# Bonus-term sums of twelve chunks moved from VectorE to TensorE, with a new instruction order

## The chip, the cores and the metric

One core of a Trainium2 chip runs the kernel. The metric is device time in microseconds (us). TensorE (PE) multiplies matrices, VectorE (DVE), ScalarE (ACT) and GpSimd (POOL) work element by element, and SyncE (SP) issues the transfers (DMA). Each engine runs its own instructions in the order in which they were written. All on-chip operands are spread over 128 partitions.

## The reference

The program is a recurrence, a mixture of attention experts and a two-layer network, for 4 batches, 8 heads, 768 time steps and 48 dimensions per head. Only the recurrence is touched:

```python
for t in range(S):
    kt, vt, rt, wt = (k[:, :, t], v[:, :, t], r[:, :, t], w[:, :, t])
    cur = np.einsum('bhd,bhe->bhde', u[None] * kt, vt)
    y[:, :, t] = np.einsum('bhd,bhde->bhe', rt, state + cur)
    state = wt[:, :, :, None] * state + np.einsum('bhd,bhe->bhde', kt, vt)
```

The part with `cur` is the bonus term. It equals v times one number for each time step and head: the sum over d of r·u·k. That number is called cb here.

## The kernel before, in words

Time is cut into chunks of 128 steps: 6 chunks for each batch, 24 in all, numbered n = 0 to 23. For each chunk SP loads w (L615), k (L623), r (L627) and v (L631) into one buffer `seq`, of which there are two. In `seq`, r, k and w lie transposed: the 48 dimensions of the even head of a pair stand in partitions 0 to 47, those of the odd head in 64 to 111, the other partitions hold zeros in r and k, and the 4 pairs times 128 steps run along the row. A further load brings r and k again in token order (128 steps in the partitions, 384 columns each) into `tok`, of which there is one (L636).

Work on a chunk:

- DVE scans the decays backward and forward (`scan` L641, `forth` L653), and multiplies them into k (`mk_k2`, L672) and r (`mk_rp`, L677).
- PE forms the scores (`mm_a`, L717), DVE copies their lower triangle (`am_copy`, L724), and PE adds the state's part (`mm_inter`, L748) and the chunk's own part (`mm_intra`, L757) into one PSUM bank `py`, of which the first 384 of 512 columns are used.
- `mm_k` (L735) transposes k, ACT copies it, `mm_d` (L766) forms the state's update, and DVE adds it (`state`, L777 and L779).
- POOL multiplies r by k in `tok` (`mk_rk`, L681) and the product by u (`mk_ruk`, L691). DVE sums each head's 48 columns (`mk_cb`, L696). POOL multiplies v by that (`mk_cv`, L701), DVE adds it to `py` (`xsum`, L786), and ACT takes absolute values for a later scale (`xabs`, L790).

A `seq` buffer is free for chunk n + 2 when `w_check`, `mm_intra`, `mm_d` and `mk_cv` of chunk n have read it.

After a batch's chunks come its projections (L874, L933), its attention (L1027 to L1135, with transposes by DMA such as `pt<-hl`) and its network (`mm_1` L1228, `mm_2` L1261). Beside the first chunks DVE also unpacks the network's weights (`decode`, L495 to L497) in two-input integer operations.

Nothing of this runs in the order of the source. A planner (class `Plan`) holds for each step an engine, a guessed duration, what it comes after and which buffers it takes and frees. It builds one order for all engines from a table `PLACE` of due times, one for each group of steps, and constants `PRM`. On PE it puts in matmuls without a use (`spin`, L587) where it expects gaps, until 208 us of its own time.

Of the kernel before, what the change touches and what calls it, by code (L numbers as in the profile page):

```python
# [9 lines left out]
F32 = mybir.dt.float32  # L10
# [49 lines left out]
    ('proj', 0): -5466.14, ('proj', 0, 1): 2505.74, ('proj', 1): 261.37, ('proj', 2): -16407.28,  # L60
# [11 lines left out]
    ('vals', 0, 1): 4670.36, ('vals', 1): 5093.45, ('vals', 2): -248.26, ('vals', 3): 10028.19, ('w1', 's'): -5079.13,  # L72
# [10 lines left out]
    'a_hi': -2276.49, 'a_lo': -4079.33, 'a_of': -4548.51, 'a_tr': -7215.53, 'ae': -2249.08, 'am_copy': -1211.61,  # L83
    'f_flag': -3788.23, 'f_rows': -3940.42, 'f_turn': -2958.01, 'forth': -7679.7, 'g_exp': -2732.59,
    'g_norm': -7208.19, 'g_rank': -1849.15, 'hi': 3513.51, 'lo': 2290.0, 'load': -15619.34, 'load_g': -1002.54,
    'load_k': -1514.23, 'load_q': -1834.95, 'load_r': 9715.31, 'load_u': -4843.94, 'load_v': -675.79, 'm_hi': 1044.13,
    'm_lo': -2041.0, 'm_out': 1738.78, 'm_store': -1805.88, 'mk': 828.69, 'mk_begin': -1810.97, 'mk_cb': 5573.98,
    'mk_cv': 1486.88, 'mk_dec': -5704.55, 'mk_k2': 14428.2, 'mk_k2t': 2766.97, 'mk_rk': 1907.93, 'mk_rp': 1676.92,
    'mk_ruk': 484.58, 'mm_1': 5584.91, 'mm_2': 2883.03, 'mm_a': 2028.85, 'mm_av': -3068.64, 'mm_d': 4246.45,
    'mm_inter': -951.53, 'mm_intra': -3321.81, 'mm_k': 4392.85, 'mm_o': -7878.45, 'mm_q': 1795.75, 'mm_s': 1704.41,  # L90
    'mm_v': -3681.48, 'mt': -1390.8, 'n_hi': -6261.32, 'n_lo': 3514.0, 'n_root': 1264.18, 'n_tr': 12577.73,
    'n_var': 2244.75, 'n_xn': -6780.08, 'o1': 1405.65, 'o2': 1686.29, 'o3': -151.85, 'o4': 5380.07, 'o5': 1003.69,
    'o_mean': 648.76, 'o_st': -1580.13, 'o_x1': 1196.05, 'q_hi': 6033.53, 'q_lo': -1025.56, 's_exp': 4056.51,
    's_hi': -10957.04, 's_lo': -1639.03, 's_max': -686.85, 's_tr': -8118.61, 'scan': -1869.51, 'se': 348.87,
    'stack': -322.35, 'state': 522.51, 'times': 1089.39, 'top': 1912.06, 'unpack': -918.54, 'v_hi': -2083.81,
    'v_lo': -2996.08, 'vc': 952.84, 'w_check': 347.52, 'ws_hi': 2045.73, 'ws_lo': -5959.97, 'ws_load': 4116.29,
    'ws_top': -14162.27, 'x_hi': 1895.35, 'x_lo': 9570.84, 'x_tr': 8171.3, 'xabs': -9224.95, 'xsum': -2843.55,
# [192 lines left out]
SPLIT = 1  # L290
RW = 384
# [12 lines left out]
def kernel(  # L304
# [68 lines left out]
    seen = const.tile([P, B * NC], F32, name="seen")  # L373
    V.memset(seen, 0.0)
    sum2 = const.tile([P, NP, max(PRM["NWA"], 1)], F32, name="sum2")
    V.memset(sum2, 0.0)
    decay = const.tile([P, B * NC, NP], F32, name="decay")
    g_sb = const.tile([P, KK], F32, name="g_sb")
    u_sb = const.tile([P, DM], F32, name="u_sb")
    spare = const.tile([P, DM], F8, name="spare")  # L380
    junk = const.tile([P, 512], F8, name="junk")
    low = const.tile([P, E, S], F16, name="low")
    G.memset(low, 0.0)
    wt = {}
    for nm, shape in (("qk", [P, 2, KK, 2 * E * HD]), ("vg", [P, 2, KK, E * HD + E]), ("wo", [P, 2, 2, DM]),
# [211 lines left out]
    def rwkv_chunk(n):  # L597
# [9 lines left out]
        def mine(tag, *more):  # L607
            return (tag, (n,) + more)
# [841 lines left out]
```

## Time and profile before

| | |
|---|---|
| three runs | 703.66, 704.58 and 707.35 us (median 704.58) |
| the profiled execution | 705.03 us, of which the span from first to last instruction is 703.3 us |
| PE matmuls | 647.3 us busy, of which 67.5 us are spins |
| DVE | 524.5 us busy |
| ACT | 396.5 us busy |
| POOL | 94.3 us busy |
| mean granted clock of PE | 0.968 |

Busy times say how much work an engine has, not which engine sets the end. That differs between stages of the span, so the rows below are given by stage. 1.7 us of the profiled execution lie outside the span.

### The profile page before, as it was taken

How to read it: one execution, taken by the hardware profiler on the slowest of the kernel's cores; microseconds unless marked ns; L12 is line 12 of the kernel's file. 1: busy time of each engine (PE TensorE's matmuls, PEld its weight loads, DVE VectorE, ACT ScalarE, POOL GpSimd, SP SyncE). 2: the span in 40 equal slices, each digit the busy share in tenths (PEclk: the TensorE clock that was granted, in tenths of full speed). 3: DMA queues.
4: the chain of work that ended last, by engine and by line, in shares of the span. 5: the costliest groups of instructions: out<-in, count | busy, mean ns of one | idle time of the engine just before them, and what ended most of it. 6: DMA issues, size and time to landing. Idle time of an engine off the chain costs nothing.

```text
span 703.3 us, 15255 instructions
## 1 busy us (share of the span) xinstructions
PE 647.3 (92%) x5599; PEld 473.9 (67%) x5606; DVE 524.5 (75%) x1321; ACT 396.5 (56%) x1176; POOL 94.3 (13%) x113
## 2 busy tenths in 40 slices
PE   7567999978899999999999999999989999999996
PEld 4444765536676786867687768577766777676773
DVE  8999898999899987887888858669764675563321
ACT  4643344879657665567584555586554576553410
POOL 4113411002222122110102200002000000000000
PEclk9867899989999999999999999999999999999998
DMA  8646566526677876756855753446674346353110
GB/s 314 205 129 213 141 156 187 196 66 140 160 165 192 165 162 148 202 92 95 187 108 145 208 126 67 84 101 156 113 118 116 73 91 120 74 79 69 31 46 28
DMA packets 173875, 92.59 MB, mean 132 GB/s; under 512 B 144736, under 2 KB 158048, under 8 KB 173792
## 3 DMA queue, kind: packets, MB, share of 16 engines
q1 hardware_dynamic: 173792, 91.53, 56.3%
q8 instruction: 46, 0.75, 0.5%
q14 instruction: 37, 0.30, 0.1%
HBM read 44.31 MB, written 4.72 MB: 70 GB/s over the span
## 4 chain that ended last, share of the span: by engine, by line
PE 56%; DVE 23%; DMA 14%; issue 3%; ACT 1%; POOL 1%; SPq 0%; DVEq 0%; POOLq 0%
PE pm L1228 16%; PE pz L1261 12%; DMA pt<-hl 7%; PE pq L874 4%; PE pv L933 3%; PE po L1083 3%; PE py L757 3%; PE px L1135 3%; PE pa L717 3%; PE spin L587 3%; DVE junk L1039 2%; DMA xT<-xs 2%; DVE hl L1061 2%; DMA seq<-in_seq_dram 2%; DVE bw L641 2%
## 5 line engine op out<-in xcount | busy, mean ns | idle before, releaser
L1228 PE MATMUL pm<-xnT,w_w 128*128 128x256 f16 x1296 | 155.5, 274 | 4.4 <-DMA xnT<-x 3.2
L1261 PE MATMUL pz<-w_w,hid 128*128 128x384 f16 x864 | 151.6, 326 | 0.6 <-DVE hid L1243 0.6
L1228 PEld LDWEIGHTS <-w_w 128*128 128x128 f16 x1296 | 123.7, 98 | 21.6 <-DMA xnT<-x 3.6
L1261 PEld LDWEIGHTS <-hid 128*128 128x128 f16 x864 | 81.8, 98 | 49.3 <-issue 0.7
L1047 ACT ACTIVATE ps<-ps,bias,scales 128x512 f32<-128x512 f32 (+3 forms) x128 | 76.7, 599 | 63.6 <-DVE junk L1039 63.2
L1039 DVE TENSOR_SCALAR_CACHE_REDUCE junk<-ps,scales 128x512 fp8e4<-128x512 f32 (+3 forms) x96 | 58.8, 613 | 22.1 <-PE ps L1028 11.7
L1061 DVE SCALAR_TENSOR_TENSOR hl<-ps,hl 128x512 f16<-128x512 f32 (+3 forms) x128 | 61.2, 501 | 16.6 <-ACT hl L1056 15.8
L587 PE MATMUL spin<-starts,ident 128*128 128x512 bf16 x241 | 67.5, 422 | 3.1 <-POOL ident masks.py:199 2.1
L1243 DVE SCALAR_TENSOR_TENSOR hid<-pm,hid 128x512 f16<-128x512 f32 x72 | 49.3, 685 | 24.5 <-ACT hid L1239 24.2
L1239 ACT ACTIVATE hid<-pm 128x512 f16<-128x512 f32 x72 | 42.6, 594 | 40.9 <-PE pm L1228 40.5
L1056 ACT ACTIVATE hl<-ps 128x512 f16<-128x512 f32 (+3 forms) x128 | 53.2, 447 | 13.3 <-DMA pt<-hl 11.9
L1083 PE MATMUL po<-vt,pt 128*128 128x64 f16 x1008 | 44.9, 194 | 12.4 <-DMA pt<-hl 12.1
L1083 PEld LDWEIGHTS <-pt 128*128 128x128 f16 x1008 | 39.7, 99 | 24.2 <-DMA pt<-hl 20.1
L874 PE MATMUL pq<-xT,w_qk 128*128 128x384 f16 x288 | 49.4, 326 | 1.2 <-DVE lg L946 0.8
L701 POOL TENSOR_TENSOR cv<-seq,cb 128x384 f32<-128x384 f32 x24 | 24.1, 1004 | 182.2 <-ACT cv L790 58.7
L757 PE MATMUL py<-seq,am 128*128 128x48 f32 x384 | 46.5, 273 | 1.8 <-DVE am L724 1.8
L757 PEld LDWEIGHTS py<-seq,am 128*128 128x128 f32 x384 | 45.5, 192 | 3.2 <-DVE am L724 2.0
L587 PEld LDWEIGHTS <-ident 128*128 128x128 bf16 x248 | 25.3, 106 | 31.7 <-issue 10.8
L1177 POOL TENSOR_TENSOR rs_y<-rs_v,half 128x2 f32<-128x2 f32 x12 | 9.5, 793 | 264.0 <-DVE rs_v L1173 264.0
L1027 PE MATMUL ps<-kd,qs 128*128 128x512 f16 (+3 forms) x128 | 39.8, 312 | 5.3 <-DVE hl L1061 5.2
L662 ACT ACTIVATE seq<-seq 128x128 f32<-128x128 f32 x96 | 28.4, 299 | 27.4 <-DVE fw L653 21.1
L681 POOL TENSOR_TENSOR tok<-tok 128x384 f32<-128x384 f32 x24 | 26.6, 1108 | 118.9 <-DMA tok<-in_tok_dram 118.9
(186 smaller groups left out, 1094.0 us busy)
## 6 DMA issues: line engine op xcount, KB each, us to landing
seq<-in_seq_dram SPq DMA_DIRECT2D x48, 256.0 KB, 4.2
tok<-in_tok_dram SPq DMA_DIRECT2D x24, 384.0 KB, 3.5
w_raw<-in_w_dram SPq DMA_DIRECT2D x24, 384.0 KB, 3.8
seq<-in_seq_dram SPq DMA_DIRECT2D x24, 258.5 KB, 2.9
seq<-in_seq_dram SPq DMA_DIRECT2D x24, 192.0 KB, 4.2
out_dram<-x SPq DMA_DIRECT2D x24, 192.0 KB, 2.1
qs<-qk SPq DMA_DIRECT2D x24, 96.0 KB, 2.1
kd<-qk SPq DMA_DIRECT2D x24, 96.0 KB, 2.2
```

The costliest lines, as they stand in the source:

```text
L587: T.matmul(bank("m", "spin"), ident16, ballast, start=True, stop=True)
L757: T.matmul(t["py"][:, h * D : (h + 1) * D], ams[h % 2][:, h // 2, :], t["vt"][:, h * D : (h + 1) * D], start=(c == 0 and h == 0), stop=(h ...
L874: T.matmul(h["pq", half][:, :384].rearrange("p (c t) -> p c t", t=P), wt["qk"][:, lw, kk, mt * P : (mt + 1) * P], t["xT"][:, 3 * half : 3 ...
L1039: V.tensor_scalar(junk[:, : k1 - k0], h["ps"][ip], t["nesc"], least[:, :1] if ip else 3.0e38, op0=OP.mult, op1=OP.min, accum_out=h["bias"] ...
L1047: A.activation(ps, ps, AF.Exp, bias=h["bias"], scale=t["esc"], accum_out=r["sums"][:, ip, e : e + 1])
L1056: A.activation(h["hl"][:, k0:k1], ps, AF.Copy, scale=2.0 ** 14)
L1061: V.scalar_tensor_tensor(out=h["hl"][:, W + k0 : W + k1], in0=ps, scalar=2.0 ** 14, in1=h["hl"][:, k0:k1], op0=OP.mult, op1=OP.subtract)
L1083: T.matmul(r["po"][:, e * HD : (e + 1) * HD], r["pt"][e][:, lp * (i + 1) + kb, :], t["vt"][:, kb, lv, e * HD : (e + 1) * HD], start=(e == ...
L1228: T.matmul(h["pm"][:, j * 256 : (j + 1) * 256].rearrange("p (c t) -> p c t", t=P), wt["w1"][:, 4 * kk + f // 3, lw, f % 3 * P : (f % 3 + 1 ...
L1239: A.activation(hid[fp][:, 0], h["pm"], AF.Relu)
L1243: V.scalar_tensor_tensor(out=hid[fp][:, 1], in0=h["pm"], scalar=0.0, in1=hid[fp][:, 0], op0=OP.max, op1=OP.subtract)
L1261: T.matmul(h["po"][:, :DM], hid[fp][:, lh, c0 : c0 + P], wt["w2"][:, 2 * fp + j, lw, :], start=(fp + j + i == 0), stop=(fp == NF // 2 - 1 ...
```

## The change

For the first 12 chunks (`REST["cb"]` is 12) the load of `tok` in token order goes, as do `mk_rk` and `mk_ruk` on 384 columns and the sum on DVE. In their place POOL multiplies the transposed r by the transposed k of `seq` once (512 columns), into the `tok` buffer. PE then multiplies each pair's 128x128 product by `usel`, a small constant that holds u of the even head in one column and u of the odd head in another, and so sums over d and multiplies by u at once. The 8 results go to unused columns of `py`, in a matmul `mm_c` that stands after `mm_intra`, and ACT copies them to `cb`. `mk_cv` and all that follows stay as they are. Two small loads bring u into `usel`, 192 elements of 4 bytes each. The other 12 chunks stay as before. The table `PLACE` is new throughout, so that the whole order can differ.

```diff
+REST = dict(w=0, x=0, q=0, st=0, xs=0, cb=12)
...
+    usel = const.tile([P, NP, 2], F32, name="usel")
+    V.memset(usel, 0.0)
+    first_u = []
...
+        paired = n < REST["cb"]
+        load_q = mk_rk = None
+        if not paired:
+          @op("SP", 0.43, follow=[load, before.get("load_q")], take=[mine("tok")], dma=copy_time(2 * DM)[1])
+          def load_q():
...
+        if paired:
+            if n == 0:
+                @op("SP", 0.86, follow=[load_v], dma=(1.8, 1.0))
+                def load_us():
+                    for j in range(2):
+                        nc.sync.dma_start(usel[64 * j : 64 * j + D, :, j],
+                                          ub[0:1, :].rearrange("a (h j d) -> j d (a h)", j=2, d=D)[j])
+
+                @op("SP", 0.43, follow=[load_us], dma=copy_time(DM)[1])
+                def load_u():
+                    nc.sync.dma_start(u_sb, ub)
+
+                first_u.append(load_us)
+
+            @op("G", 1.35, after=[load_k, load_r], take=[mine("tok")])
+            def mk_rk():
+                t["q"] = buf("tok", [P, 2, DM], F32, f"tok_{nm}").rearrange("p a b -> p (a b)")[:, : NP * P].rearrange("p (h t) -> p h t", t=P)
+                G.tensor_tensor(out=t["q"], in0=t["rT"], in1=t["kT"], op=OP.mult)
...
+        if paired:
+            @op("PE", 0.9, dense=0.5, after=[mk_rk] + first_u, follow=[mm_intra], free=[mine("tok")])
+            def mm_c():
+                for hp in range(NP):
+                    T.matmul(t["py"][:, DM + 2 * hp : DM + 2 * hp + 2], t["q"][:, hp, :], usel[:, hp, :],
+                             start=False, stop=True, skip_group_check=True)
+
+            @op("A", 0.24, after=[mm_c])
+            def mk_cb():
+                t["cb"] = small("cb", [P, H], f"cb_{nm}", 4)
+                A.activation(t["cb"], t["py"][:, DM : DM + H], AF.Copy)
+
+        @op("G", 0.83, after=[mk_cb, load_v], follow=[before.get("cv")], take=[mine("cv")], free=[mine("seq")])
+        def mk_cv():
```

## Rows read from the trace of the kernel before

**Rows 1.** The page: busy time of an engine, share of the span, instructions; then its slices.

```profile
PE 647.3 (92%) x5599; PEld 473.9 (67%) x5606; DVE 524.5 (75%) x1321; ACT 396.5 (56%) x1176; POOL 94.3 (13%) x113
...
DVE  8999898999899987887888858669764675563321
```

**Rows 2.** By stage: PE, PEld, DVE, ACT, POOL busy (x instructions), PEclk, DMA share, GB/s.

```profile
0.00:14.00 14.00, 10.47 (x56) 5.37 (x57) 12.19 (x26) 5.40 (x22) 7.71 (x19) 1.00 0.87 301
14.00:165.00 151.00, 124.55 (x827) 82.15 (x832) 138.94 (x325) 85.92 (x298) 30.35 (x27) 0.88 0.59 166
165.00:200.00 35.00, 30.14 (x256) 21.76 (x254) 31.66 (x78) 26.48 (x80) 7.89 (x8) 0.95 0.67 169
200.00:703.00 503.00, 482.08 (x4471) 364.61 (x4469) 341.73 (x894) 278.66 (x779) 48.39 (x59) 1.00 0.55 114
```

**Rows 3.** The same view for one short stretch.

```profile
68.50:74.50 6.00, 6.00 (x35) 5.11 (x36) 5.96 (x10) 2.34 (x5) 1.63 (x1) 0.50 0.70 158
```

**Rows 4.** The chain that ended last: start, us, what.

```profile
15.78 0.47 DVE cb L696
...
78.93 4.71 PE spin L587 x21
...
88.45 4.37 DMA seq<-in_seq_dram
92.92 1.23 DVE bw L641
...
157.37 0.46 DVE cb L696
```

**Rows 5.** Groups by line: busy us, mean ns of one, idle time before them and its releaser.

```profile
L662 ACT ACTIVATE seq<-seq 128x128 f32<-128x128 f32 x96 | 28.4, 299 | 27.4 <-DVE fw L653 21.1 <-issue 4.5 <-PE pk L735 1.3
...
L701 POOL TENSOR_TENSOR cv<-seq,cb 128x384 f32<-128x384 f32 x24 | 24.1, 1004 | 182.2 <-ACT cv L790 58.7 <-ACT hl L1056 34.3 <-DVE cb L696 29.1
...
L696 DVE TENSOR_REDUCE cb<-tok 128x8 f32<-128x384 f32 x24 | 13.0, 544 | 2.2 <-POOL tok L691 2.2
...
L979 ACT ACTIVATE gex<-gex 128x24 f32<-128x24 f32 (+1 forms) x5 | 1.1, 215 | 6.8 <-DVE gex L975 6.8
```

**Rows 6.** The instructions of `tok` up to 206 us: ns min/median/max, first and last start.

```profile
L681 POOL TENSOR_TENSOR tok<-tok x12: 994/998/1680, 6.2 to 196.1; 128x384 f32<-128x384 f32 x12
L691 POOL TENSOR_TENSOR tok<-tok,u_sb x12: 994/1124/1486, 9.3 to 197.2; 128x384 f32<-128x384 f32 x12
```

**Rows 7.** Timeline of DVE: start, us, instruction.

```profile
6.78 0.93 DVE L672 TENSOR_TENSOR k<-seq,bw 128x512 f32<-128x512 f32 x1 [0.55 <-DMA seq<-in_seq_dram]
...
19.32 0.56 DVE L496 SCALAR_TENSOR_TENSOR w_w<-w_raw,w_w 128x384 int32<-128x384 int32 x1
...
20.78 1.31 DVE L496 SCALAR_TENSOR_TENSOR w_w<-w_raw,w_w 128x384 int32<-128x384 int32 x1
22.13 1.24 DVE L497 SCALAR_TENSOR_TENSOR w_w<-w_raw,w_w 128x384 int32<-128x384 int32 x1
...
197.36 0.81 DVE L1102 TENSOR_TENSOR den<-den,gw 128x4 f32<-128x4 f32 x1
```

**Rows 8.** Timeline of POOL beside them.

```profile
20.68 1.00 POOL L681 TENSOR_TENSOR tok<-tok 128x384 f32<-128x384 f32 x1 [3.54 <-DMA tok<-in_tok_dram]
21.76 1.19 POOL L691 TENSOR_TENSOR tok<-tok,u_sb 128x384 f32<-128x384 f32 x1
```

**Rows 9.** Timeline of PE, SP and DVE around one release of `seq`.

```profile
86.50 1.88 PE L757 MATMUL py<-seq,am 128*128 128x48 f32 x16
...
88.45 0.47 SPq L615 DMA_DIRECT2D seq<-in_seq_dram  x1
...
92.92 1.23 DVE L641 TENSOR_TENSOR_SCAN bw<-seq,starts 128x516 f32<-128x516 f32 x1 [0.29 <-DMA seq<-in_seq_dram]
```

**Rows 10.** DMA issues: count, KB each, median us to landing.

```profile
tok<-in_tok_dram SPq DMA_DIRECT2D x24, 384.0 KB, 3.5
...
g_sb<-in_gln_dram SPq DMA_DIRECT2D x1, 1.5 KB, 6.0
```

More of the change, by code (lines that the diff above doesn't have):

```diff
@@ L39 @@
 PLACE = {
[20 rows of a table removed]
-    ('proj', 0): -5466.14, ('proj', 0, 1): 2505.74, ('proj', 1): 261.37, ('proj', 2): -16407.28,
[11 rows of a table removed]
-    ('vals', 0, 1): 4670.36, ('vals', 1): 5093.45, ('vals', 2): -248.26, ('vals', 3): 10028.19, ('w1', 's'): -5079.13,
[10 rows of a table removed]
-    'a_hi': -2276.49, 'a_lo': -4079.33, 'a_of': -4548.51, 'a_tr': -7215.53, 'ae': -2249.08, 'am_copy': -1211.61,
-    'f_flag': -3788.23, 'f_rows': -3940.42, 'f_turn': -2958.01, 'forth': -7679.7, 'g_exp': -2732.59,
-    'g_norm': -7208.19, 'g_rank': -1849.15, 'hi': 3513.51, 'lo': 2290.0, 'load': -15619.34, 'load_g': -1002.54,
@@ L86 @@
[L86 to L95, printed above, removed]
@@ L96 @@
-    'v_lo': -2996.08, 'vc': 952.84, 'w_check': 347.52, 'ws_hi': 2045.73, 'ws_lo': -5959.97, 'ws_load': 4116.29,
-    'ws_top': -14162.27, 'x_hi': 1895.35, 'x_lo': 9570.84, 'x_tr': 8171.3, 'xabs': -9224.95, 'xsum': -2843.55,
[20 rows of a table added]
+    ('proj', 0, 1): 766.82, ('proj', 1): 1638.04, ('proj', 2): -19323.32, ('proj', 3): 5337.8, ('rw', 0): -10712.38,
[10 rows of a table added]
+    ('s', 3, 5): -5179.54, ('small',): -5254.12, ('vals', 0): -398.28, ('vals', 0, 1): 2431.17, ('vals', 1): 3339.14,
[10 rows of a table added]
+    ('w2', 8): -5346.35, ('w2', 9): -6391.77, 'a_den': 10744.99, 'a_hi': -4707.8, 'a_lo': -223.93, 'a_of': -2880.19,
@@ new lines @@
+    'a_tr': -5821.5, 'ae': -2155.34, 'am_copy': -1064.51, 'f_flag': -3115.11, 'f_rows': -7491.3, 'f_turn': -2172.62,
+    'forth': -7694.37, 'g_exp': -5909.91, 'g_norm': -5522.85, 'g_rank': -2505.22, 'hi': 3755.67, 'lo': 1990.61,
+    'load': -16103.1, 'load_g': -1748.33, 'load_k': -661.45, 'load_q': -7397.01, 'load_r': 9252.29,
+    'load_u': -3214.49, 'load_us': 791.32, 'load_v': -106.46, 'm_hi': 2417.99, 'm_lo': -1788.18, 'm_out': 1503.45,
+    'm_store': 1417.58, 'mk': 591.07, 'mk_begin': -1404.74, 'mk_cb': 8255.22, 'mk_cv': 1530.44, 'mk_dec': -1979.53,
@@ new lines @@
+    'mk_k2': 13875.77, 'mk_k2t': 3972.17, 'mk_rk': 2927.76, 'mk_rp': -77.92, 'mk_ruk': 526.26, 'mm_1': 6481.26,
+    'mm_2': 3428.07, 'mm_a': 1461.31, 'mm_av': -3852.14, 'mm_c': 588.86, 'mm_d': 4149.33, 'mm_inter': 98.01,
+    'mm_intra': -1673.8, 'mm_k': 3224.36, 'mm_o': -11419.26, 'mm_q': 1630.25, 'mm_s': 1461.83, 'mm_v': -2282.4,
+    'mt': -1351.68, 'n_hi': -4961.3, 'n_lo': 2777.16, 'n_root': 1257.35, 'n_tr': 15167.33, 'n_var': 1448.05,
+    'n_xn': -5556.28, 'o1': 1107.48, 'o2': 1489.72, 'o3': -2784.3, 'o4': 2902.6, 'o5': 2361.7, 'o_mean': 1006.31,
@@ new lines @@
+    'o_st': -1951.96, 'o_x1': 733.94, 'q_hi': 4654.5, 'q_lo': -1355.91, 's_exp': 4045.38, 's_hi': -9233.33,
+    's_lo': -3309.39, 's_max': -8.84, 's_tr': -7583.32, 'scan': -1467.7, 'se': 30.4, 'stack': -3588.09,
+    'state': -729.19, 'times': 1590.36, 'top': -118.98, 'unpack': -2801.37, 'v_hi': -3961.17, 'v_lo': -4106.49,
+    'vc': 2924.17, 'w_check': 736.18, 'ws_hi': 3483.43, 'ws_lo': -3109.71, 'ws_load': 4669.5, 'ws_top': -12025.52,
+    'x_hi': 1885.36, 'x_lo': 8317.75, 'x_tr': 10822.11, 'xabs': -10303.95, 'xsum': -2421.49,
@@ L631, in load_v @@
             nc.sync.dma_start(t["vt"], seq[n, :, OFF_TV : OFF_TV + DM])
-        @op("SP", 0.43, follow=[load, before.get("load_q")], take=[mine("tok")], dma=copy_time(2 * DM)[1])
-        def load_q():
+        paired = n < REST["cb"]
[3 more added lines that the diff above has]
+          def load_q():
             t["q"] = buf("tok", [P, 2, DM], F32, f"tok_{nm}")
@@ L677, in mk_rp @@
             V.tensor_tensor(out=t["rp"], in0=t["rT"], in1=t["fw"][:, :, :P], op=OP.mult)
-        @op("G", 1.01, after=[load_q])
-        def mk_rk():
-            G.tensor_tensor(out=t["q"][:, 0], in0=t["q"][:, 0], in1=t["q"][:, 1], op=OP.mult)
-        load_u = None
-        if n == 0:
-            @op("SP", 0.43, follow=[load_v], dma=copy_time(DM)[1])
-            def load_u():
-                nc.sync.dma_start(u_sb, ub)
-        @op("G", 1.01, after=[mk_rk, load_u])
-        def mk_ruk():
-            G.tensor_tensor(out=t["q"][:, 0], in0=t["q"][:, 0], in1=u_sb, op=OP.mult)
@@ L693, in mk_cb, with mk_rk, load_u, mk_ruk @@
-        @op("V", 0.54, after=[mk_ruk], free=[mine("tok")])
-        def mk_cb():
-            t["cb"] = small("cb", [P, H], f"cb_{nm}", 4)
-            V.tensor_reduce(out=t["cb"], in_=t["q"][:, 0].rearrange("p (h d) -> p h d", d=D), axis=AX.X, op=OP.add)
-        @op("G", 0.83, after=[mk_cb, load_v], follow=[before.get("cv")], take=[mine("cv")], free=[mine("seq")])
-        def mk_cv():
-            t["cv"] = buf("cv", [P, H, D], F32, f"cv_{nm}")
-            G.tensor_tensor(out=t["cv"], in0=t["vt"].rearrange("p (h d) -> p h d", d=D),
-                            in1=t["cb"][:, :, None].to_broadcast([P, H, D]), op=OP.mult)
+        if paired:
[13 more added lines that the diff above has]
+                G.tensor_tensor(out=t["q"], in0=t["rT"], in1=t["kT"], op=OP.mult)
+        else:
+            @op("G", 1.01, after=[load_q])
+            def mk_rk():
+                G.tensor_tensor(out=t["q"][:, 0], in0=t["q"][:, 0], in1=t["q"][:, 1], op=OP.mult)
+            load_u = None
+            if n == 0:
+                @op("SP", 0.43, follow=[load_v], dma=copy_time(DM)[1])
+                def load_u():
+                    nc.sync.dma_start(u_sb, ub)
+            @op("G", 1.01, after=[mk_rk, load_u])
+            def mk_ruk():
+                G.tensor_tensor(out=t["q"][:, 0], in0=t["q"][:, 0], in1=u_sb, op=OP.mult)
+            @op("V", 0.54, after=[mk_ruk], free=[mine("tok")])
+            def mk_cb():
+                t["cb"] = small("cb", [P, H], f"cb_{nm}", 4)
+                V.tensor_reduce(out=t["cb"], in_=t["q"][:, 0].rearrange("p (h d) -> p h d", d=D), axis=AX.X, op=OP.add)
@@ L758, in mm_intra, with mk_cb @@
                          start=(c == 0 and h == 0), stop=(h == H - 1), skip_group_check=True)
+        if paired:
[5 more added lines that the diff above has]
+            @op("A", 0.24, after=[mm_c])
+            def mk_cb():
+                t["cb"] = small("cb", [P, H], f"cb_{nm}", 4)
+                A.activation(t["cb"], t["py"][:, DM : DM + H], AF.Copy)
+        @op("G", 0.83, after=[mk_cb, load_v], follow=[before.get("cv")], take=[mine("cv")], free=[mine("seq")])
+        def mk_cv():
+            t["cv"] = buf("cv", [P, H, D], F32, f"cv_{nm}")
+            G.tensor_tensor(out=t["cv"], in0=t["vt"].rearrange("p (h d) -> p h d", d=D),
+                            in1=t["cb"][:, :, None].to_broadcast([P, H, D]), op=OP.mult)
         state = None
```

81 rows, old and new, of the table PLACE are left out of this document.

## The prediction

> **What bounds the kernel now.** Start with the page's busy times and the slices of DVE [rows 1]. PE is busy for 92% of the span, which looks like the end of the matter. But the slices show DVE at 8 to 9 tenths in the first quarter and falling later, so the stages must be read apart. The busy time by stage [rows 2] does that. From 14 to 165 us DVE is busy for 138.94 of 151 us. From 200 us on it is PE, with 482.08 of 503. PE's early business is in good part the spins, which the table above puts at 67.5 us. So DVE paces the front, and PE's own work paces the rest. Whatever brings the front to its end sooner brings all that follows forward, as the work of the second part does not grow.
>
> The chain that ended last [rows 4] agrees. Up to 165 us it runs mostly on DVE (its DVE pieces from 13.7 to 165 us, added up, are 86 of 151 us, 57%), among them the sum `mk_cb`: six of its pieces between 15.78 and 157.37 us, 2.4 us together. The rest of that stretch is PE with spins among its work (4.71 us of them at 78.93), a load of `seq` at 88.45, and some transposes by DMA.
>
> A third thing is seen only in single instructions [rows 7, 8]. The weights' unpacking step L496 takes 0.56 us alone, but 1.31 us at 20.78, and L497 1.24 us at 22.13, while POOL multiplies in `tok` (20.68 to 22.95). POOL's products hold up DVE's two-input instructions.
>
> **What goes.** Twelve sums on DVE at 0.544 us [rows 5] are 6.5 us. Twelve first and twelve second products on POOL go too (their medians are 0.998 and 1.124 us [rows 6]). With them goes what they cost DVE. I compared every DVE instruction up to 206 us that lies over these 24 products with the unstretched time of its form. 15 are longer, from L672 at 6.78 us (0.93 against 0.68) to L1102 at 197.36 us (0.81 against 0.16) [rows 7], by 9.4 us in all. Twelve loads of 384 KB go [rows 10], most of them hidden today. The first stands ahead of the first k, r and v, when the queues run at 301 GB/s [rows 2], so it is 1.3 us of transfer, and the full u (192 KB) now need not come early: 0.6 us. DVE idles 14.0 - 12.19 = 1.8 us in that stage [rows 2], so the start gains between 0 and 1.8 us. I take half, 0.9.
>
> **What comes.** POOL's new product has 512 columns in place of 384: 0.998 x 512/384 = 1.33 us [rows 6], 12 x 1.33 = 16 us. No row shows it. It can hit a DVE instruction with two inputs or none. The 24 old products were busy for some 27 us and stretched DVE by 9.4, or 0.35 us for each us of POOL. At that rate the new ones cost 16 x 0.35 = 5.6. The bounds are 0 (all fall beside one-input work) and 12 x 1.33 x 0.75 = 12 (all do as L496 did at 20.78 [rows 7, 8]). I take 5.6, because where they fall is open and the mean of 24 cases is the nearest row.
>
> PE gets four products of a 128x128 weight per chunk. Eight such, with 48 columns, took 1.88 us in `mm_intra` [rows 9], so four are at most 0.94 us. Two columns for 48 may make it less, but the weights must be loaded all the same. Up to 200 us there are spins to give way (4.71 us in one piece [rows 4]), so most of this is hidden. Without that cover it is 12 x 0.94 = 11 us. I charge one chunk before 165 us and the last (n = 11, at 211 us, where PE has no idle time): 1.8 us, between 0.9 and 3.8 + 0.9. ACT gets 12 copies of 8 columns at about 0.215 us [rows 5], 2.6 us. ACT is busy 85.92 of 151 us [rows 2], so nothing for the work itself. What queues behind a copy is the next evacuation of a bank, and PE waits for that only if the copy itself waits for `mm_c`.
>
> The order around `mk_cv` changes. cb no longer comes from its own load, ahead of the recurrence, but from behind `mm_intra`: `mm_c` 0.94, the copy 0.215, `mk_cv` 1.0 [rows 5, 9], 2.2 us in all before `seq` is free. SP's load of the next chunk but one stands behind that, and all loads and transposes later in SP's queue stand behind it too. Today such a load leaves right when `mm_intra` has ended: that of 86.50 us ends at 88.38, the load starts at 88.45, and the scan starts when it has landed, at 92.92, DVE having idled 0.29 us [rows 9], on the chain [rows 4]. This one could be 2.2 us later. DVE may have other work for part of it: 0 to 2.2, I take 1.1. For chunks where cb was the late one, as the 29.1 us that `mk_cv` waited for DVE show [rows 5], the load leaves earlier. I count nothing for that, since DVE is busy then anyway. `xsum` waits for `mk_cv` too, but DVE, being busy, mostly comes to it later than that, so nothing there.
>
> **The sum.** Up to 165 us DVE loses nine sums (4.9 us) and, outside the start, some 7.2 us of stretch, and gains eight products' worth, 8 x 1.33 x 0.35 = 3.7: 8.4 us of relief. If only the part on the chain counts, 57%, that is 4.8 us. If DVE is refilled as today, 92%, it is 7.7. The order is new, so the chain of today is no sure guide, and DVE was refilled well: I take the middle, 6.3. Then -6.3 - 0.9 + 1.8 + 1.1 = -4.3 us. The span goes from 703.3 to 699.0 us, and the profiled execution from 705.03 to 700.7. That execution was 0.45 us above the median, so I forecast 700.3 us. The smallest change that I would tell from none is 0.5%, 3.5 us.
>
> **A page's rule on the loads of `usel`.** The only tiny load of today, `g_sb`, 1.5 KB in 128 pieces of 12 bytes, took 6.0 us to land [rows 10], behind other loads. The two new loads together have 384 pieces of 4 bytes. The Trainium skill ("DMA: Bandwidth & Descriptors", section "Rules for kernel authors") says that a strided last dimension becomes one descriptor per element and should be rearranged. That speaks against these loads, and no run here shows their cost. By it the sum would be that of the third rival below, -1.3.
>
> **Rivals.** *The front is not shortened where it counts (0.27 with the third rival).* The relief turns into waiting: for the transposes on the chain, for spins that the new order puts ahead of real work, or for PE at half its clock. From 68.5 to 74.5 us the granted clock was 0.50 (1.2 GHz), PE was busy all 6 us [rows 3] and on the chain. One more such stretch of 6 us costs 3 us. For it speaks that 43% of the chain up to 165 us is not on DVE. Against it, that DVE has idled only 12 us there [rows 2]. With the start's 0.9 and the 4.8 on the chain less 3 for the clock and 1.8 for PE, this gives -0.9: 703.7 us.
>
> *The late release of `seq` decides: slower (0.23).* Place: the loads for chunks 6, 7, 8, 11 and 13, which today leave within a few us of `mm_intra` or `mm_d`. Each comes 2.2 us later. Where the copy queues on ACT behind the four squares and their reads of `w_check` (4 x 0.49 us, of which 0.299 are the square [rows 5]), it is 4.1 us. For it: one such load is on the chain today [rows 9]. Against it: the order may put other DVE work there, and cb comes earlier where it was late. It decides once these delays pass 6.3 + 0.9 - 1.8 = 5.4 us. With three at 4.1 and no other change the time is 704.6 - 5.4 + 12.3 = 711.5, with four at 2.2 it is 708.0.
>
> *The loads of `usel` land late.* Three times the pieces of `g_sb`, at three times its 6.0 us [rows 10], is 18 us. Issued with the first chunk's loads, at about 3.6 us, they land at 21.6, where `mm_intra` of chunk 0 ends at 16.5. That chunk's `mk_cv` and its `seq` come 5 us late, of which the 2 us that DVE does not fill remain, and the start's gain is lost: -4.3 + 3 = -1.3, or 703.3 us. Against it: `g_sb` waited behind four loads of weights, so its own share of the 6.0 us is smaller. 0.04 of the 0.27.
>
> **How the numbers follow.** Forecast 0.50, front not shortened or `usel` late 0.27, `seq` late 0.23. So faster by over 0.5% 0.50, within it 0.27, slower 0.23. The low end takes the sums of all twelve chunks (6.5), the stretch at its mean saving (3.8), and the whole start (1.8), less the last `mm_c`: -11.2, or 693.4. With fewer hits of the new products it is lower, so 691. The high end is the second rival, 708 to 711.5: 711. Its worst cases and a part of the new order's own luck stay out. The forecast's own range is 694 to 701.
>
> **What would show it.** The group L696 should have 12 instructions in place of 24, and POOL 12 products of some 1.33 us. DVE's busy time should fall by about 10 us (6.5 + 3.8). The unpacking steps should be stretched less often. The first `pm` matmul of L1228, at 190 us today, should come 4 to 6 us earlier, and everything behind it by as much. PE's busy time should hold about 0.9 us of `mm_c` per chunk and fewer spins. The prediction is wrong if that first matmul comes at the same time, if DVE's waits for `seq` grow past 5 us, if PE's clock before 200 us falls below today's 0.88 [rows 2], or if the new order loses in the second part what the front gained.

## The result, and the profile after

The changed kernel is slower: 715.00 us (median of 4 runs, 711.65 to 718.49) against 704.27 before, a ratio of 1.0148 [1.0111, 1.0186]. 700.3 was forecast. Ratios leave out the few runs that lie over 1.5% above the fastest of their kernel (two of eight for the kernel with chunk 0's product first); medians hold them. The profiled execution, 718.49 us with a span of 716.7, is the slowest of the four: it is 13.5 us above the profiled one before, where the medians are 10.7 apart. Its page, with the same lines as [rows 1] and the granted clock by slices:

```profile
PE 659.9 (92%) x5657; PEld 490.6 (68%) x5665; DVE 511.9 (71%) x1310; ACT 396.3 (55%) x1188; POOL 83.2 (12%) x101
...
DVE  7898976998688898678886895877454566564321
PEclk9865558999999999999999999999999999999999
```

DVE lost 12.6 us of work, and PE gained 12.6. By stage from 14 us on, against [rows 2]:

```profile
14.00:165.00 151.00, 123.05 (x761) 88.31 (x765) 127.29 (x306) 87.31 (x303) 21.49 (x18) 0.75 0.47 133
165.00:200.00 35.00, 34.08 (x302) 25.14 (x305) 26.20 (x66) 21.30 (x72) 5.84 (x7) 1.00 0.66 143
200.00:716.00 516.00, 492.45 (x4539) 371.39 (x4536) 346.13 (x913) 282.93 (x794) 48.93 (x59) 0.99 0.55 114
```

The granted clock of 14 to 165 us fell from 0.88 to 0.75. The first `pm` matmul (L1270) starts at 203.35 us, before at 189.99. From there to the end of the span it is 513.3 us in both. In these two executions all of the loss lies ahead of it. The groups of the new work, and the spins:

```profile
L594 PE MATMUL spin<-starts,ident 128*128 128x512 bf16 x203 | 58.7, 421 | 3.2 <-POOL ident masks.py:199 2.1
...
L706 POOL TENSOR_TENSOR tok<-seq 128x512 f32<-128x512 f32 x12 | 18.4, 1532 | 72.5 <-DMA seq<-in_seq_dram 22.5 <-PE ps L1071 14.1 <-issue 13.8
L788 PE MATMUL py<-usel,tok 128*128 128x2 f32 x96 | 13.8, 266 | 0.3 <-POOL tok L706 0.3
...
L726 DVE TENSOR_REDUCE cb<-tok 128x8 f32<-128x384 f32 x12 | 6.6, 547 | 0.1
L794 ACT ACTIVATE cb<-py 128x8 f32<-128x8 f32 x12 | 2.0, 171 | 17.2 <-PE py L788 17.2
```

PE issues 38 spins fewer and is still 12.6 us busier. The sums `mm_c` are 13.8 us of it, and ACT stood idle for 17.2 us in all ahead of the copies, which waited for them. Where the front goes wrong is seen in the timelines from 9 to 56 us (start, us, instruction), first that of POOL:

```profile
9.55 1.64 POOL L706 TENSOR_TENSOR tok<-seq 128x512 f32<-128x512 f32 x1 [3.34 <-DMA seq<-in_seq_dram]
24.99 1.27 POOL L706 TENSOR_TENSOR tok<-seq 128x512 f32<-128x512 f32 x1 [13.80 <-issue]
27.66 0.99 POOL L799 TENSOR_TENSOR cv<-seq,cb 128x384 f32<-128x384 f32 x1 [1.40 <-ACT cb L794]
...
38.10 1.01 POOL L799 TENSOR_TENSOR cv<-seq,cb 128x384 f32<-128x384 f32 x1
```

of PE, the sums:

```profile
23.84 1.02 PE L788 MATMUL py<-usel,tok 128*128 128x2 f32 x8
26.32 1.05 PE L788 MATMUL py<-usel,tok 128*128 128x2 f32 x8 [0.27 <-POOL tok L706]
```

of SP:

```profile
20.83 9.28 SPq L527 DMA_DIRECT2D w_raw<-in_w_dram  x5
30.20 0.38 SPq L622 DMA_DIRECT2D seq<-in_seq_dram  x1
...
36.50 19.05 SPq L527 DMA_DIRECT2D w_raw<-in_w_dram  x7
55.65 0.37 SPq L622 DMA_DIRECT2D seq<-in_seq_dram  x1
```

and of SP in the kernel before:

```profile
17.17 0.33 SPq L615 DMA_DIRECT2D seq<-in_seq_dram  x1
...
33.52 0.33 SPq L615 DMA_DIRECT2D seq<-in_seq_dram  x1
```

The product at 9.55 us is that of chunk 1. There is one `tok` buffer (`tok=1` in SIZES) and nothing orders the product of a chunk behind that of the chunk before, so the order gave the buffer to chunk 1 first. Chunk 0's product stood until the sums of chunk 1 (23.84) had read it, and started at 24.99. Its own sums are at 26.32, its `mk_cv` at 27.66, and only when that ends, at 28.65, is its `seq` free (before at 17.14). The load of chunk 2, which also stands behind five loads of weights, leaves at 30.20, where it left at 17.17 before. Chunk 3's buffer is free when chunk 1's `mk_cv` ends, at 39.1 (before at 33.50), but its load stands behind seven loads of weights in SP's queue and leaves at 55.65, before at 33.52. So most of chunk 2's delay is the late release of `seq`, and 16.5 of chunk 3's 22.1 us are its place in the queue. The chain that ended last shows what the loads of weights waited for (start, us, what):

```profile
24.00 0.85 PE py L788 x8
...
51.30 1.65 PE py L788 x8
...
52.97 0.04 ACT cb L794
...
53.49 0.20 ACT w_raw L398
...
53.70 3.22 DMA w_raw<-in_w_dram
```

The sums of chunk 2 take 1.65 us at half clock (those of chunk 1 took 0.85 at full clock), ACT's copy waits for them (5.12 us in the timeline), ACT's square sums L398 stand behind the copy, and a load of weights waits for the buffer that they empty. From 60.1 to 77.5 us PE has nothing but waiting, and the granted clock stays at 0.50 (1.2 GHz) for 61 us. The same stretch before, and here:

```profile
42.50:104.00 61.50, 53.89 (x345) 37.00 (x347) 56.36 (x108) 25.37 (x96) 18.17 (x15) 0.82 0.59 158
...
42.50:104.00 61.50, 39.84 (x178) 30.45 (x180) 53.38 (x121) 32.14 (x99) 5.29 (x4) 0.50 0.46 145
```

### The profile page after: what moved, and what is told of

Its sections match the earlier page's. It is cut to its first block, busy times and chain, and to the rows that moved or that the text cites. A ratio compares the mean times of both kernels' runs of the same rounds, so it can differ in the third digit from the quotient of the medians.

```text
span 716.7 us, 15331 instructions
## 1 busy us (share of the span) xinstructions
PE 659.9 (92%) x5657; PEld 490.6 (68%) x5665; DVE 511.9 (71%) x1310; ACT 396.3 (55%) x1188; POOL 83.2 (12%) x101
## 4 chain that ended last, share of the span: by engine, by line
PE 63%; DVE 15%; DMA 15%; ACT 3%; issue 3%; SPq 1%; POOL 0%; DVEq 0%; ACTq 0%
PE pm L1270 16%; PE pz L1303 14%; DMA pt<-hl 9%; PE pq L916 5%; PE py L781 5%; PE spin L594 3%; DMA seq<-in_seq_dram 3%; PE po L1125 3%; PE pv L975 3%; PE pa L741 3%; PE px L1177 2%; PE py L772 2%; DVE junk L1081 2%; PE ps L1069 2%; DVE hl L1103 1%
## 5 line engine op out<-in xcount | busy, mean ns | idle before, releaser
L1270 PE MATMUL pm<-xnT,w_w 128*128 128x256 f16 x1296 | 155.6, 274 | 0.6 <-DMA xnT<-x 0.5
L1270 PEld LDWEIGHTS <-w_w 128*128 128x128 f16 x1296 | 124.1, 98 | 16.0 <-issue 0.9
L594 PE MATMUL spin<-starts,ident 128*128 128x512 bf16 x203 | 58.7, 421 | 3.2 <-POOL ident masks.py:199 2.1
L916 PE MATMUL pq<-xT,w_qk 128*128 128x384 f16 x288 | 51.7, 333 | 0.5 <-DVE qk L935 0.4
L781 PE MATMUL py<-seq,am 128*128 128x48 f32 x384 | 49.7, 285 | 0.4 <-DVE am L748 0.3
L781 PEld LDWEIGHTS py<-seq,am 128*128 128x128 f32 x384 | 48.5, 204 | 1.8 <-DVE am L748 1.0
L594 PEld LDWEIGHTS <-ident 128*128 128x128 bf16 x211 | 21.2, 104 | 30.2 <-issue 13.2
L916 PEld LDWEIGHTS <-w_qk 128*128 128x128 f16 x288 | 28.5, 100 | 19.5 <-issue 2.6
L748 DVE COPY_PREDICATED am<-above,pa 128x512 f32<-128x512 int8 x48 | 33.4, 721 | 10.3 <-PE pa L741 9.9
```

Of the source, the lines that this page charges most:

```text
L594: T.matmul(bank("m", "spin"), ident16, ballast, start=True, stop=True)
L781: T.matmul(t["py"][:, h * D : (h + 1) * D], ams[h % 2][:, h // 2, :], t["vt"][:, h * D : (h + 1) * D], start=(c == 0 and h == 0), stop=(h ...
L916: T.matmul(h["pq", half][:, :384].rearrange("p (c t) -> p c t", t=P), wt["qk"][:, lw, kk, mt * P : (mt + 1) * P], t["xT"][:, 3 * half : 3 ...
L1270: T.matmul(h["pm"][:, j * 256 : (j + 1) * 256].rearrange("p (c t) -> p c t", t=P), wt["w1"][:, 4 * kk + f // 3, lw, f % 3 * P : (f % 3 + 1 ...
```

## The experiments

Theory 1: the new work is light enough, and the order around the first chunks (the only `tok` buffer, SP's queue) makes the front late. Theory 2: the new work itself costs, by the passes on TensorE or by the chain sums, copy, value product. Most kernels run a written list in place of the planner's order; only the list differs then:

```diff
-        for o in self.order(look, late, warm):
...
+        for i in ORDER if warm else ():
+            (warm["run"] if i < 0 else self.ops[i].run)()
+        for o in () if warm else self.order(look, late, warm):
             o.run()
```

**The old work at the new places** (`load_q` beside the chunk's load, `mk_ruk` behind `mk_rk`).

> The reverse: the work of the kernel before (load in token order, two products on GpSimd, the sum on VectorE), with every step at its place in the changed kernel's order. Theory A (the order): 712 to 722 us, since the order's late loads of chunks 2 and 3 stay and VectorE has its sums back. Theory B (the work): 703 to 708 us.

736.51 us, ratio 1.0461 [1.0429, 1.0493], above the ranges of both theories.

**The new work at the old places**, chunk 0's product ahead of chunk 1's, `mm_c` behind `mm_intra`:

> The changed work in the order of the kernel before: every step keeps its place, the product of r and k stands where a chunk's backward product with k stood, the sums on TensorE right behind the chunk's own part, the copy on ScalarE about 1 us later, and what depends on them moves back only as far as it must. Theory A (the new order made the time worse, the work itself is lighter): 694 to 702 us, with the first network matmul (first pm) at 183 to 190 us. Theory B (the changed work itself, through the later release of seq, made it worse): 708 to 716 us, first pm at 195 to 205 us.

715.60 us, ratio 1.0173 [1.0135, 1.0212]. The time is theory B's and the first `pm`, at 189.18 us, theory A's. It is as early as before, but from there to the end it is 523.7 us and not 513.3: the time is lost behind it, at the seam between the new and the old form. The x sum (`xsum`) of chunk 10 starts at 194.2 us (193.7 before), that of chunk 11 at 223.7 (213.6). The only `tok` buffer is free for chunk 12's tokens when chunk 11's sums have read it, and on POOL chunk 11's value product stands in line behind chunk 12's two products, which wait for that load. The timeline of SP in this kernel:

```profile
214.36 0.33 SPq L650 DMA_DIRECT2D tok<-in_tok_dram  x1
```

and that of POOL:

```profile
217.48 0.99 POOL L715 TENSOR_TENSOR tok<-tok 128x384 f32<-128x384 f32 x1 [24.43 <-DMA tok<-in_tok_dram]
218.55 0.99 POOL L725 TENSOR_TENSOR tok<-tok,u_sb 128x384 f32<-128x384 f32 x1
219.50 0.82 POOL L803 TENSOR_TENSOR cv<-seq,cb 128x384 f32<-128x384 f32 x1
```

So each order is bad for the other's work, and this pair alone decides nothing.

**More spins in the changed kernel**, 60 ahead of the transpose that PE waited for at 77.5 us.

> The changed kernel with 60 more spins on TensorE in one place: where it stood idle for 17.6 us before the scale of the first projection, at 60 to 78 us. Theory C (the 61 us at half the clock are the loss): the granted clock is 1.00 from about 70 us on, the first network matmul comes 8 to 13 us earlier than 203 us, and the time is 702 to 708 us. Theory A or B (the chunks come late, and the clock only follows from that): the clock rises as well, but the first network matmul comes less than 4 us earlier, and the time is 711 to 715 us.

713.79 us, ratio 1.0159 [1.0120, 1.0198], no gain (the median is 1.2 us lower, the ratio higher). The spins lifted the clock, but only while they ran, as the busy times by stretch show (columns as in [rows 2]):

```profile
60.00:70.00 10.00, 10.00 (x48) 4.46 (x47) 9.83 (x20) 9.33 (x30) 0.61 (x1) 1.00 0.41 139
70.00:75.00 5.00, 2.95 (x26) 1.50 (x24) 4.86 (x12) 5.00 (x15) 0.00 (x0) 1.00 0.75 227
75.00:80.00 5.00, 4.28 (x21) 3.77 (x19) 4.93 (x11) 3.37 (x13) 0.00 (x0) 0.53 0.51 168
...
80.00:100.00 20.00, 19.38 (x83) 12.91 (x82) 15.83 (x38) 7.91 (x24) 2.36 (x2) 0.52 0.26 70
```

The recurrence's products behind the spins ran at 0.5 again. So this run does not tell what the half clock costs. It tells something else: up to 55 us its order is that of the changed kernel, yet chunk 2's load leaves at 28.22 and chunk 3's at 51.62 us, and the first `pm` starts at 194.67, in an execution of 710.63 us. So some 2 and 4 us of the delays read above belong to that one execution, and its 203.35 us is a poor mark to judge single moves by.

**Chunk 0's product first**, its sums, copy, value product and x sum right behind, and chunk 2's load ahead of five loads of weights; all else as in the changed kernel. The two engines' lists in outline:

```diff
 GpSimd, SyncE:
-  product(1) ... sums(1) ... product(0), cv(0) ... w_raw x5, load(2)
+  product(0), product(1), cv(0) ... load(2), w_raw x5
```

> The changed kernel, in which chunk 0's product on GpSimd goes ahead of chunk 1's, its sums follow at once, and the load of chunk 2 stands ahead of five loads of weights. Nothing else moves. Theory B in its narrow form (the one tok buffer, given to chunk 1 first, makes chunk 0's seq and so chunk 2's load late): chunk 2's load starts at about 18 us in place of 30, and the time is 4 to 9 us below the changed kernel, 706 to 711 us. Theory A: the rest of the order keeps VectorE's sequence and chunk 3's load at 55 us, so the gain is under 3 us, 712 to 716 us.

709.66 us (704.03 to 715.32), ratio 1.0041 [1.0002, 1.0081]. By the ratio 1.1 points of the loss of 1.5% go with this one move, by the medians 5.3 of 10.7 us. The first `pm` is at 194.10, no earlier than in the run with spins. SP's queue shows chunk 2 leaving early, chunk 3 still behind weights, although its buffer is free at 26.22:

```profile
17.99 0.33 SPq L626 DMA_DIRECT2D seq<-in_seq_dram  x1
...
21.81 28.46 SPq L531 DMA_DIRECT2D w_raw<-in_w_dram  x12
50.36 0.38 SPq L626 DMA_DIRECT2D seq<-in_seq_dram  x1
```

**The old places with the seam mended**: chunk 11's copy and value product ahead of chunk 12's products on POOL, chunk 12's reduction behind chunk 11's `xsum`.

> The changed work in the order of the kernel before, as in e3_old_order, but with the seam between chunk 11 and chunk 12 mended: the copy and the value product of chunk 11 stand ahead of the token-order products of chunk 12 on GpSimd, and the reduction of chunk 12 stands on VectorE after the x sum of chunk 11, ahead of the scan of chunk 13. No operation is added or left out. Theory 1 (the new work is no heavier than the old; the loss of the changed kernel is the front, where the only tok buffer goes to chunk 1 first): the x sum of chunk 11 returns from 223.72 us of e3_old_order to about 214, the stretch from the first state product to the end from 523.7 to about 513, and the time falls by some 8 to 10 us against e3_old_order, to 702 to 707 us, level with the kernel before. Rival (the added passes on TensorE and the longer GpSimd product cost what they take, wherever they stand): the time stays at 710 us or above although the seam is mended, with the loss spread over the chunks.

709.35 us, ratio 1.0074 [1.0046, 1.0101]: theory 1's 702 to 707 missed. The first `pm` is at 190.05, as before. This is a look at the forecast's main term in an order that did not change, though PE has more work in it. PE, PEld, DVE, ACT and POOL busy from 14 to 100 us, first in the kernel before:

```profile
14.00:100.00 86.00, 68.26 (x439) 48.08 (x440) 79.43 (x160) 41.02 (x161) 21.87 (x19) 0.82 0.62 179
```

and here:

```profile
14.00:100.00 86.00, 74.31 (x473) 55.70 (x472) 68.07 (x149) 40.64 (x164) 15.35 (x13) 0.78 0.50 148
```

DVE is relieved of 11.4 of its 79.4 us, PE gets 6 us more, and the front ends no sooner. DVE waits more; the wait that grew most from 14 to 200 us (us, times, longest), in the kernel before:

```profile
DVE xf L786 <- POOL cv L701: 1.7, 2, 0.9
```

and here:

```profile
DVE xf L832 <- POOL cv L803: 8.5, 4, 3.8
```

The loss is behind the front. The x sum of chunk 10 is 1.4 us later than before (195.1 against 193.7), that of chunk 12 4.8 us (247.5 against 242.7), that of chunk 23 4.9: most of it comes in at the seam, which the edit mended in part.

**One constraint for the planner**, with the new and with the old table of places:

```diff
-            @op("G", 1.35, after=[load_k, load_r], take=[mine("tok")])
+            @op("G", 1.35, after=[load_k, load_r], follow=[before.get("rk")], take=[mine("tok")])
```

> The changed kernel with one constraint more: the product of r and k of a chunk follows that of the chunk before it, so that chunk 0 gets the only tok buffer before chunk 1; the order is drawn up anew under it from the same table of places. Theory 1 (the order of the two first products is what makes the front late): the load of chunk 2 leaves at 17 to 20 us instead of 30.20, that of chunk 3 before 40 instead of at 55.65, the first state product starts at 188 to 193 us instead of 203.35, and the time is 700 to 706 us. Theory 2 (the front is late by the loads in SyncE's queue behind weight loads, whichever chunk gets tok first): chunk 2 is early, chunk 3 stays at 50 us or later, and the time is near 709.7 us, that of e4_first_product. Theory 3 (the added work itself): 712 us or more.

> As f1_follow, with the table of places of the kernel before in place of the new one. If the order of the first products decides, it is within 4 us of f1_follow, at 700 to 707 us, with the load of chunk 2 at 17 to 20 us. If the new table is what costs (the rival that the place of everything else decides), it is faster than f1_follow by 5 us or more; if the new table is needed by the new work, slower by as much.

724.06 us, 1.0270 [1.0222, 1.0319], and 732.05, 1.0371 [1.0324, 1.0419]. Both times missed far. The old table is 8.0 us slower than the new one, the last of the cases named: the new work needs the new table. In the first, chunk 2's load leaves at 20.97 us, chunk 3's at 30.73, and the first `pm` starts at 169.83, 20 us earlier than before. But PE then lacks work: it is busy for 39.13 of the 50 us from 100 to 150 (44.65 before), and for 41.70 from 200 to 250 (47.32). An early first `pm` is no proof of a short front, and a table of places fits one set of constraints.

**The sums ahead of `mm_intra`, the passes doubled, and spins in the fourth kernel.** In the second, `for hp in range(NP)` of `mm_c` becomes `for hp in [*range(NP)] * 2`; the other two kernels move entries of the list or add spins to it.

> As e3b_seam, but in the ten chunks that are not the first of a batch row the sums on TensorE stand right behind the inter-chunk product, ahead of the intra-chunk product, and the copy and the value product follow some 2 us later in the order; nothing else is moved. In e3b_seam VectorE waited 8.5 us for the value product (4 times, longest 3.8) between 14 and 200 us, against 1.7 us in the kernel before, and the x sums of chunks 11 and 12 came 3.5 and 4.8 us later than before. Theory 1 (what is left of the loss in e3b_seam is that the bonus now follows the intra-chunk product in series: sums, copy, value product, x sum, and holds tok until then): VectorE's wait for the value product falls under 3 us, the x sum of chunk 11 comes at or before 214 us, and the time is 701 to 705 us. Rival (the passes cost TensorE their time wherever they stand): 708 us or more, with the waits gone but the x sums no earlier.

> As e3b_seam with each of the twelve chunks' eight passes of the sums issued twice into the same columns, so that the bonus is taken twice and the output is not the reference's; 96 passes more. Eight passes took 0.85 us at full clock and 1.63 at half. Theory 1 (the passes stand on the path that sets the end, in the front as elsewhere): 10 to 14 us more than e3b_seam, 719 to 723 us. Theory 2 (in the front TensorE waits for other things anyway, and the passes take that time): 0 to 4 us more, 709 to 713 us.

> e4_first_product (chunk 0's product before chunk 1's, 709.66 us) with spins added on TensorE ahead of two transposes that it waited for: 14 ahead of that of a weight's maximum at 50.66 us and 56 ahead of that of the first projection's scale at 71.04 us; there TensorE was idle for 5.7 and 16.2 us, and its clock at half until 97 us. Theory 1 (the late front and the half clock add up to the whole loss of the changed kernel): the granted clock of 55 to 75 us is 1.00, the first state product starts some 5 us earlier than e4_first_product's 194.1, and the time is 703 to 707 us. Rival (the clock falls again at the small recurrence matmuls and the added spins stand in the way): 709 us or more.

The first: 711.36 us, 1.0101 [1.0066, 1.0136], no better than behind `mm_intra` (DVE still waited 7.3 us for the value product, and 9.8 for `pd`, 5.9 in the mended kernel). The second: 719.90 us, 1.0220 [1.0177, 1.0262], 1.5 points or some 10 us over the mended kernel for 96 passes more, as theory 1 had it. The third: 713.15 us, 1.0111 [1.0062, 1.0161], no gain. From 55 to 75 us its clock was 0.88, from 75 to 80 us 0.68.

**Fewer and cheaper passes**, in the mended kernel: one product of eight columns for four of two, and the product of r and k in 16 bits.

```diff
-t["q"] = buf("tok", [P, 2, DM], F32, ...)
+t["q"] = buf("tok", [P, NP, P], F16, ...)
+if n == 0:
+    G.tensor_copy(usel16, usel)
...
-T.matmul(t["py"][...], t["q"][:, hp, :], usel[:, hp, :], ...)
+T.matmul(t["py"][...], t["q"][:, hp, :], usel16[:, hp, :], ...)
```

> As e3b_seam, but each chunk's sums are one product over the first of the four pairs of heads in place of four products: 24 passes on TensorE in place of 96, so that the bonus of six heads is not the reference's. Doubling the passes added 10.5 us for 96 (719.90 against 709.35). Theory 1 (each pass stands on the path at some 0.11 us, and beside that the changed work is lighter by some 5 us): 72 passes fewer take 7 to 9 us off, 700 to 703 us, at or below the kernel before. Rival (the passes cost only where they are added to a full engine, and the serial chain of sums, copy and value product is what costs): 706 us or more.

> As e3b_seam, but GpSimd writes the product of r and k in 16 bits (f16), and the copy of u that TensorE takes is f16 too (one small copy on GpSimd in chunk 0): 48 passes in place of 96, and weight loads that took 98 ns where f32 ones took 206. Theory 1 (the price of the change on TensorE is loading the product as f32 weights): the sums' busy time falls from 13.2 us to under 6, and the time by 5 to 8 us against e3b_seam, to 701 to 704 us, level with the kernel before or a little better. Rival (the latency of the chain, not TensorE's time): within 2 us of e3b_seam.

A quarter of the passes: 707.64 us, 1.0052 [1.0032, 1.0072], only 1.7 us off where 7 to 9 were expected. 16 bits: 704.75 us, 1.0021 [1.0000, 1.0042], 4.6 us off, just short of the 5 to 8 expected and level with the kernel before. The groups of the sums and their weight loads, in the mended kernel:

```profile
L792 PE MATMUL py<-usel,tok 128*128 128x2 f32 x96 | 13.2, 259 | 0.0
...
L792 PEld LDWEIGHTS py<-usel,tok 128*128 128x128 f32 x96 | 12.7, 206 | 0.0
```

and in 16 bits:

```profile
L795 PE MATMUL py<-usel,tok 128*128 128x2 f16 x48 | 2.9, 165 | 0.0
...
L795 PEld LDWEIGHTS <-tok 128*128 128x128 f16 x48 | 3.3, 118 | 0.0
```

The Trainium skill ("TensorE: Matmul & The Clock Gate", section "Weight-path perf modes — Fast Weight Load (FWL) and DoubleRow") says that weights of 128 columns load by a faster way unless they are FP32. The trace agrees: 118 ns against 206, for half as many loads.

With the passes doubled and quartered the same order tells what they cost in the front. The first `pm`, in the kernel before, with 24, with 96 and with 192 passes:

```profile
189.99 1.16 PE L1228 MATMUL pm<-xnT,w_w 128*128 128x256 f16 x9 [3.25 <-DMA xnT<-x]
...
185.33 1.16 PE L1273 MATMUL pm<-xnT,w_w 128*128 128x256 f16 x9 [1.11 <-DMA xnT<-x]
...
190.05 1.16 PE L1274 MATMUL pm<-xnT,w_w 128*128 128x256 f16 x9 [1.18 <-DMA xnT<-x]
...
198.02 1.15 PE L1274 MATMUL pm<-xnT,w_w 128*128 128x256 f16 x9
```

The step from 24 to 96 passes costs 4.7 us, that from 96 to 192 8.0. Carried down to no passes, the front would end at about 183.8 us, 6.2 ahead of the kernel before: an estimate from one execution each, where two executions of the same order (the 16-bit kernel and the next one, up to chunk 10) differ by up to 2.1 us in their x sums. By it DVE's relief was there, and the passes ate it; whether by PE's time or by the longer chain the runs do not part. Behind the front it is lost in another way: with a quarter of the passes chunk 10's x sum is 3.6 us earlier than before (190.1), chunk 12's 2.6 us later (245.3).

**The seam by itself, and 16 bits in the two other orders.**

> As e17_half_precision, but chunk 11's sums stand right behind its inter-chunk product, the token-order load of chunk 12 right behind them in SyncE's queue, and the copy and value product of chunk 11 ahead of its intra-chunk product. Theory 1 (what is left of the loss in the order of the kernel before is the seam): the load of chunk 12's tokens leaves at or before 207 us instead of 210.68, the x sum of chunk 12 comes at 239 to 242 us instead of 244.60, and the time is 699 to 703 us, faster than the kernel before. Rival (the seam is hidden and the leftover lies in the projections behind it): 704 to 706 us, as e17_half_precision.

> The order of e4_first_product with the product of r and k and the copy of u in f16 (48 passes in place of 96, f16 weight loads). Theory 1 (in this order the sums also stand on the path, at half clock in the front, at about 1.6 us a chunk): 4 to 7 us less than e4_first_product, 703 to 706 us. Rival (chunk 3's late load sets the front there, and the sums are hidden behind it): 707 to 710 us.

> The changed kernel in its own order, with the product of r and k and the copy of u in f16 and nothing else. If the price of the sums on TensorE is the larger part of its loss, it falls by 7 us or more, to 708 us or less. If the late front is (theory 1), by 2 to 6 us, to 709 to 713 us, with the load of chunk 2 still at 29 us or later.

The seam: chunk 12's tokens left at 208.63 us in place of 210.68, not at 207 or before, chunk 12's x sum came at 245.4 us, not at 239 to 242, and the time is 706.28 us, 1.0028 [1.0008, 1.0049], no gain. 16 bits with chunk 0 first: 710.31 us, 1.0084 [1.0055, 1.0112]. 16 bits in the changed kernel alone: 710.42 us, 1.0094 [1.0075, 1.0114], 0.5 points better than the changed kernel, with chunk 2's load still at 28.72. With chunk 0 first, 16 bits bring nothing more. No version here beats the kernel before; the 16-bit one at the old places comes level with it.

Four of the runs cross order and precision (ratios):

| | f32 | 16 bits |
|---|---|---|
| the new order | 1.0148 | 1.0094 |
| the old places, seam mended | 1.0074 | 1.0021 |

16 bits take off 0.5 points in either order, and the old places 0.7 points in either precision. By the intervals above each of these differences is uncertain by some 0.3 to 0.5 points. What remains is 0.2 points.

## Why the prediction was wrong

Two terms of the sum were mis-sized, PE's 1.8 us and the 1.1 us for the release of `seq`, and for what the new order itself loses the sum had no term.

PE's term of 1.8 us rested on spins giving way. The price of one chunk was right (0.85 us at full clock, at most 0.94 forecast) but is 1.65 at half clock, and the cover was not there: with 38 spins fewer PE is 12.6 us busier. In either order f32 costs 0.5 points, 3.8 us, more than 16 bits do, and at the old places the last 72 of the 96 passes alone bring the first `pm` 4.7 us later. The bound given for the cover gone, 11 us, is about what doubling the passes cost. A quarter of them saves only 1.7 us in the end, as the rest goes at the seam.

The new order costs 0.7 points, 5 us, against the old places. Its front holds the late loads, and the second rival had a part of their mechanism, with the wrong place and size. It named the loads of chunks 6, 7, 8, 11 and 13 at 2.2 to 4.1 us each; at the old places in f32 they leave -0.2, 2.5, 0.6, 0.0 and 5.2 us later than before. In the profiled execution of the changed kernel it was chunk 2's, 13.0 us late, and chunk 3's, 22.1. Of that, 11.5 and 5.6 us are the late release of `seq`; the rest is SP's queue, where the new order has weights ahead of them. What I did not read is who holds `tok`: it used to be filled by a load that ran ahead of the recurrence, now from `mk_rk` to `mm_c`, and it is a single buffer without an order between chunks. Giving it to chunk 0 first took 1.1 of the 1.5 points in f32, but 0.1 in 16 bits (1.0094 to 1.0084), so its share of the loss is not shown.

The sum's -6.3 was right in DVE's busy time (12.6 us less work, about 10 forecast; 12 reductions in L726). Its premise "DVE paces the front" left out that the same change gives PE, at half its clock for part of the front, more to do there: at the old places the front ended at the same time (190.05 against 189.99 us), and 4.7 us earlier with a quarter of the passes. No run shows the relief at the end. The sentence "`xsum` waits for `mk_cv` too ... so nothing there" was wrong: that wait grew from 1.7 to 8.5 us. The start's 0.9 did not come either; chunk 0's x sum is at 18.0 us at the old places, at 17.2 before.

The first rival's clock came about, for 61 us and not six; what it cost no run shows, as the added spins did not lift it for the products behind them. The third rival did not: the loads of `usel` landed after 4.3 and 4.5 us (18 were feared), so the strided rows, against which the Trainium skill speaks ("DMA: Bandwidth & Descriptors", section "Rules for kernel authors"), cost nothing that the time shows. ACT's copy was priced at 0.215 us and took 0.171, but "only if the copy itself waits for `mm_c`" became the rule: 17.2 us, longest 5.12, with the weights' square sums behind it. POOL's product took 1.37 us in the median, 1.53 in the mean (1.33 forecast). One reading was too narrow: not only two-input instructions are held up, as the one-input L1100 took 0.75 us at 196.36, beside POOL's product at 196.09, and 0.16 in its median. That the second part does not grow was right for the changed kernel, 513.3 us in both, and not for the old places (517.6 in f32).

Open: what is lost between chunk 10 and chunk 12 at the old places, why the order with chunk 0 first gains nothing by 16 bits, and which part of the new order costs its 0.7 points. Chunk 3's load behind twelve loads of weights is seen there; moving it was not tried.

## What to carry to other kernels

A buffer that is moved from a load ahead of the work to the middle of the work is held much longer: before costing the operations, write down for each single buffer who holds it from when to when, and which two users can come in the wrong order. The release of a chunk's input is the place to look at in the first chunks, where one late load meets a queue full of other loads. When work moves from one engine to another, run the same order with less and with more of it on the engine that takes it, before a new order is drawn up: that parts the relief from its price. Where a change has two parts, here order and precision, run all four combinations. And carry no table of places from one set of constraints to another.

## What was unexpected of the hardware

A busy PE was no sign of the upper clock. With 60 spins the granted clock was 1.00 (2.4 GHz) from 60 to 75 us, although PE was busy for only 2.95 of the last 5. From 80 to 100 us, where the recurrence's f32 products ran and 12 spins among them, it was 0.52, close to the lower level (1.2 GHz), with PE busy for 19.38 of 20 us. Passes of two columns cost almost what those of 48 cost: in the changed kernel at full clock eight of two columns took 1.02 us and sixteen of 48 took 1.91, at half clock 1.83 and 3.49. Both load weights of 128 columns, and 16-bit weights bring a pass of two columns from 259 to 165 ns; that the weights set the price is inferred from this. And GpSimd's product of 512 columns varied from 1.27 to 2.50 us.
